# A Mamba-2 block and a gated feed-forward on one core: four first products ahead of the state products, three behind, and two of three copies by VectorE

## The chip, the cores and the metric

The kernel runs on one core of one Trainium2 chip. The metric is the device time of one execution in microseconds. The kernel before was timed in three runs: 345.36, 347.25 and 347.58 us, median 347.25 us. One further execution was taken with the hardware profiler. It took 349.48 us, of which 347.8 us are the profile's span (first to last instruction); all times inside the kernel are counted from the span's start.

## The reference

Two parts follow each other. The first is a state-space recurrence over 32 sequences (4 batches x 8 heads) of 768 positions, with head size 32 and state size 16; the second is a feed-forward over the resulting 3072 tokens of 256 channels.

```python
for c in range(nc):                        # chunks of 32 positions
    cum = np.cumsum(la, axis=-1)           # la = log(clip(a, 1e-6, 1))
    L = np.exp(cum[:, :, :, None] - cum[:, :, None, :]) * causal
    M = np.einsum('bhin,bhjn->bhij', Cc, Bc) * L
    y_intra = np.einsum('bhij,bhjd->bhid', M, xc)
    y_inter = np.einsum('bhin,bhnd->bhid', Cc, state) * np.exp(cum)[:, :, :, None]
    y[:, :, sl] = y_intra + y_inter
    state = decay_full * state + sum_j(B_j x_j * decay_from_j)
# tokens (3072, 256) = y, heads side by side
h = x @ w_in                               # 256 -> 2048
g = h * (1.0 / (1.0 + np.exp(-1.702 * h)))
out = g @ w_out                            # 2048 -> 256
```

The weights come as float64; the kernel makes float32 of their bits.

## The kernel before, in words

**Tiling.** The 3072 tokens are cut into six groups of 512. A group is two "pairs"; a pair is two chunks of 128 positions, each computed as two sides of 64. For each group the kernel makes yT, the recurrence's output with channels on partitions ([128, 2, 512]), then the hidden layer and the output. The code counts groups from 0 (g); this text says group 1 to group 6. In the loop over g from 2 to 4, the feed-forward of group g+1 is computed while the recurrence of group g+2 is prepared, so the three passes of that loop make the yT of groups 4, 5 and 6.

**The recurrence of one group** has these steps: `score` (the products of C and B into PSUM, tile cb, L677), `weigh` (VectorE multiplies the decay L by cb, L688), `finish` (the products y: first those with the carried state, L817, then those within the side, L831, in all 368 or 384 instructions of TensorE, half of them weight loads), and the copies of y from PSUM into yT. For groups 4 to 6 (`swap`, code groups above 2), the halves of the second side lie exchanged in PSUM, so three copies are needed: one of 128x512 (L866) and two of 64x512 (L864) which go from partitions 64 to 127 into 0 to 63 and the other way. All three are on ScalarE.

**The feed-forward** multiplies 2x2 blocks with seven products in place of eight. For each of eight steps j, the first layer has seven "first" products, which the code calls j.1 to j.7. Products 1, 6, 7, 4 add up in one PSUM tile X (L947), in that order, and ScalarE copies X out after 1, 6 and 7 (L952) and takes the silu after 4. Products 5, 2, 3 add up in Y (L957); VectorE adds the copies to Y (L1079: j.D after 5 and 2, and another one after 3), and ScalarE takes the silu of the sums (L924: j.S, j.T). `mix_g` (M0, M1 and so on; L915 to L917) makes the sums and differences of a finished step for the second layer, and P is one of the seven products of the second layer (L1052), added up over all j in the tile acc. Each such product is two weight loads and two matmuls in the profile.

**PSUM.** X and Y take turns in four banks. The tiles cb, y and acc take turns in one area of four banks: y can be written only when `weigh` has read cb, and acc only when the three copies have read y.

**What sets the order.** `run(g, steps)` emits the steps of a string from left to right, and `in_order` at the end fixes this order on each engine. Waits between engines come from the tiles that they share. The string around the change is the one of `more` in the loop over groups. In it s is `score`, w `weigh`, y `finish` with its copies, and `refill` starts the loads of the next pair: a memset of one element by VectorE (L267), behind which SP issues the DMAs of a (decay, from scratch), af, zC, zB, b and x. The a that it loads is read by VectorE's scan (`decay`, L419) at the end of the string.

Of the kernel before, what the change touches and what calls it, by code (L numbers as in the profile page):

```python
# [11 lines left out]
AF = mybir.ActivationFunctionType  # L12
# [4 lines left out]
P = 128  # L17
# [18 lines left out]
def kernel(  # L36
# [31 lines left out]
    nc = tc.nc  # L68
# [218 lines left out]
    for r in range(R):  # L287
        (nc.sync, nc.scalar)[r % 2].dma_start(
            out=az0[32 * r:32 * r + 32].rearrange("p k s -> p (k s)"),
# [493 lines left out]
    def finish(pairs, steps=range(2)):  # L783


        g, first = divmod(pairs[0], PG)
        early = pairs[0] < PG

        swap = g > 2
        if 0 in steps:  # L790
            if early:
                y = [bank(f"y0_{i}")[:, :2 * P].rearrange("p (k i) -> p k i", i=H) for i in range(4)]
                begun_y[0] = [[y[2 * t + i] for t in range(NK)] for i in range(2)], set()
            else:
                both = area(f"y{pairs[0]}")[:, :, :len(pairs) * 2 * H].rearrange(
                    "p (s t) (k i) -> p s t k i", s=2, i=H)
                begun_y[pairs[0]] = [[both[:, i, t] for t in range(NK)] for i in range(2)] + [both], set()
        y, begun = begun_y[pairs[0]]

        def begin(i, t, parts):  # L800
            new = not begun & {(i, t, q) for q in parts}
            begun.update((i, t, q) for q in parts)
            return new

        def inter(n, p, sides=range(2)):

            for k in range(2):
                for i in sides:
                    m = 2 * k + i
                    if (4 * p + m) % (2 * NC) == 0:  # L810
                        continue
                    old = state[p][:, m - 1] if m else state[p - 1][:, 3]
                    for r in range(R):
                        t = r // 2
                        half = r % 2 ^ (swap and i)
                        rows, to = slice(32 * r, 32 * r + 32), Q * D * half
                        nc.tensor.matmul(  # L817
                            out=y[i][t][to:to + Q * D, 2 * n + k], lhsT=old[rows],
                            rhs=st[p]["CsT"][rows, k, SIDES[i]],
                            start=begin(i, t, range(Q * half, Q * half + Q)), stop=early,  # L820
                            tile_position=(32 * r, to), skip_group_check=True)

        def intra(n, p):
            L = Ls[p]
            for h, k in [(h, k) for h in range(NH) for k in range(2)] if early else [
                    (h, k) for k in range(2) for h in range(NH)]:
                    for i, side in enumerate(SIDES):
                        t, q = divmod(h, HB)
                        if i and swap:
                            q = (q + Q) % HB  # L830
                        nc.tensor.matmul(  # L831
                            out=y[i][t][D * q:D * q + D, 2 * n + k], lhsT=rx[p][side, k, h],
                            rhs=L[side, k, h // Q, h % Q],
                            start=begin(i, t, (q,)), stop=not early, tile_position=(H * i, D * q),
                            skip_group_check=True)

        cols = slice(2 * first * P, 2 * (first + len(pairs)) * P)

        if first == 0:
            yT[g] = ffn.tile([P, NK, TG], FP32, tag="yT", name=f"yT{g}")  # L840
        if early:
            for n, p in enumerate(pairs):
                if n:
                    fan_all(PG)
                intra(n, p)
            for n, p in enumerate(pairs):
                for i in range(2):
                    inter(n, p, (i,))
            for t in range(NK):
                for i in range(2):  # L850
                    nc.scalar.activation(  # L851
                        yT[g][:, t, cols].rearrange("p (k s i) -> p s k i", s=2, i=H)[:, i], y[i][t],
                        AF.Copy)
        else:
            for step in steps:
                for n, p in enumerate(pairs):
                    (inter, intra)[step](n, p)
            if 1 not in steps:
                return
            o = yT[g][:, :, cols].rearrange("p t (k s i) -> p s t k i", s=2, i=H)  # L860
            for i in range(2):
                if i and swap:
                    for to, src in (SIDES, SIDES[::-1]):
                        nc.scalar.activation(o[to, i], y[2][src, i], AF.Copy)  # L864
                else:
                    nc.scalar.activation(o[:, i], y[2][:, i], AF.Copy)  # L866
        for p in pairs:
            state.pop(p - 1, None)
            st.pop(p)
            Ls.pop(p)  # L870
# [313 lines left out]
    to = area("cb0")  # L1184
# [99 lines left out]
    def run(g, steps, products=(), **do):  # L1284


        products = iter(products)
        for step in steps.split():
            if step == "P":
                product(*next(products))  # L1290
            elif step in do:
                do[step]()
            else:
                j, i = step.split(".")
                first(g, int(j), i)
        assert next(products, None) is None
# [52 lines left out]
    for g in range(2, NG):  # L1349
        n, p = (g + 1) * PG, (g + 2) * PG  # L1350
        more, most = g + 1 < NG, g + 2 < NG
        rows = [b for b in range(NB) if most and (g + 2) * CG <= b * NC < (g + 3) * CG]
        if most:
            load(p)
        run(g, "0.1 P P 0.6 P P 0.7 P 0.5 P 0.2 P 0.D", seven(g - 1, 6))
        def turn_third():
            if g == 2:
                turn_blocks(3)

        def start_third():  # L1360
            if g == 2:
                for k in n, n + 1:
                    since_start(k)

        def mask_third(k):
            if g == 2:
                mask_blocks(k)

        left = []
        run(g, "1.1 t 0.S P 0.4 P P 1.6 u P 0.3 b 0.T v P 1.5 P 1.7 1.2 P 1.D C", seven(g - 1, 7),  # L1370
            C=lambda: left.append(combine(g - 1)), t=turn_third, b=start_third,
            u=lambda: mask_third(n), v=lambda: mask_third(n + 1))
        def along():
            for r in rows:
                clip_rows(r)
                decay_rows(r)

        def refill():
            if most:
                spread(p, held=True)  # L1380
                for b in rows:
                    spread_rows(b)
                load(p + 1)
                spread(p + 1)

        if more:

            run(g, "2.1 1.S 1.4 1.3 2.6 2.5 2.2 2.7 1.T 3.1 s 2.D 2.S w 2.4 2.3 3.6 M0 3.5 3.2 3.7 2.T y "
                "refill 3.D 4.1 4.5 4.2 3.4 3.3 P P 4.6 P 3.S P 3.T M1 4.7 P P P 4.D M2",
                seven(g, 0), s=lambda: score((n, n + 1)), w=lambda: (weigh(n), weigh(n + 1)),  # L1390
                y=lambda: finish((n, n + 1)), refill=refill,
                M0=lambda: mix_g(g, 0), M1=lambda: mix_g(g, 1), M2=lambda: mix_g(g, 2))
            if most:
                decay(p)
        else:
            run(g, "2.1 1.S 1.4 1.3 2.6 2.5 2.2 2.7 1.T 2.D M0 3.1 3.5 2.4 3.6 2.S 2.3 Z 3.2 3.7 2.T 3.D M1",
                M0=lambda: mix_g(g, 0), M1=lambda: mix_g(g, 1), Z=lambda: left.pop()())
        for j in range(5 if more else 4, NF // 2):
            if j == 5:
                do = lambda: (mix_g(g, 3), turn_out(g - 1, 0))  # L1400
            else:
                do = lambda: mix_g(g, j - 2)
            run(g, steady(j, "o" if j == 6 else ""), seven(g, j - 4), M=do,
                o=lambda: turn_out(g - 1, 1))
            if most and j == 5:
                along()
            if most and j == 6:
                decay(p + 1)
            if most and j == 7:
                turn_blocks(g + 2)  # L1410
        k = NF // 2 - 1
        run(g, closing(k), seven(g, 4))
        if not more:
            for j in range(k - 1, k + 1):
                mix_g(g, j)
            break
        mix_g(g, 6)

        run(g, "P P A P P P P P", seven(g, 5), A=lambda: ahead(g + 1, p if most else None))
        mix_g(g, 7)  # L1420
# [33 lines left out]
```

## Time and profile before

| what | before |
|---|---|
| runs | 345.36, 347.25, 347.58 us; median 347.25 us |
| profiled execution | 349.48 us, span 347.8 us |
| TensorE busy | 340.9 us (98%) |
| TensorE weight loads busy | 272.9 us (78%, beside the matmuls) |
| VectorE busy | 256.1 us (74%) |
| ScalarE busy | 155.0 us (45%) |
| GpSimd busy | 14.4 us (4%) |
| granted TensorE clock, mean | 0.995 |

A busy share is an average over the whole span. What a stage is worth is read from that stage: from which wait ends last there. A line such as L947 is a line of the kernel; "PEld" is TensorE's weight load, "PE" its matmul, DVE is VectorE, ACT is ScalarE, SP issues most DMAs. An fp32 product shows as two matmuls and two weight loads in the trace.

### The profile page before, as it was taken

The page shows a single profiled execution, that of the slowest core. Times are in us where ns is not written, and L with a number is a line of the kernel's source. Part 1 is how long each engine was busy: PE and PEld are TensorE (multiplying, and loading weights), DVE is VectorE, ACT ScalarE, POOL GpSimd, SP SyncE. Part 2 cuts the span into 40 slices and gives each one's busy share as a digit, 9 for nine tenths or more (in the row PEclk, how much of TensorE's full clock was granted, in tenths as well). Part 3 has the DMA queues.
Part 4 walks back from the last instruction along what each step waited for, and adds up shares of the span by engine and source line. Part 5 has one row for each costly group of instructions (what it writes and reads, how often), then busy time and mean ns, then how long its engine had stood idle before and what let it go on. Part 6 is the DMA issues. An engine that isn't in the chain of part 4 may idle for free.

```text
span 347.8 us, 8119 instructions
## 1 busy us (share of the span) xinstructions
PE 340.9 (98%) x3378; PEld 272.9 (78%) x3378; DVE 256.1 (74%) x486; ACT 155.0 (45%) x353; POOL 14.4 (4%) x40
## 2 busy tenths in 40 slices
PE   8999999999999999979999999999999999999996
PEld 6644744555788888868888888888888888899996
DVE  6889999999998897837996567788464654465463
ACT  5797672316543315534442554432554321554320
POOL 6100111100000000000000000000000000000000
PEclk9999999999999999989999999999999999999999
DMA  6698899755736001346404016400000300000401
GB/s 163 153 285 195 243 206 132 149 79 110 115 95 114 0 2 30 47 123 106 78 19 59 0 62 121 80 0 3 0 4 3 60 2 0 0 2 0 62 0 61
DMA packets 89972, 25.75 MB, mean 74 GB/s; under 512 B 73392, under 2 KB 87216, under 8 KB 89936
## 3 DMA queue, kind: packets, MB, share of 16 engines
q1 hardware_dynamic: 89104, 24.72, 34.8%
q10 hardware_dynamic: 832, 0.52, 0.6%
q8 instruction: 26, 0.43, 0.5%
q14 instruction: 10, 0.08, 0.1%
HBM read 21.99 MB, written 3.24 MB: 73 GB/s over the span
## 4 chain that ended last, share of the span: by engine, by line
PE 98%; issue 1%; ACT 0%; DVE 0%
PE acc L1052 28%; PE X L947 19%; PE Y L957 14%; PE h L891 10%; PE o L989 8%; PE acc L1059 7%; PE y L831 3%; PE cb L677 2%; PE y L817 1%; PE A L708 1%; PE ab L551 1%; PE busy L463 1%; PE ab L545 0%; PE tp L594 0%; ACT yT L851 0%
## 5 line engine op out<-in xcount | busy, mean ns | idle before, releaser
L952 ACT ACTIVATE ac<-X 128x256 f32<-128x256 f32 x76 | 29.1, 383 | 82.9 <-PE X L947 82.5
L1079 DVE TENSOR_TENSOR gT<-Y,ac 128x512 f32<-128x512 f32 x38 | 26.2, 689 | 38.6 <-PE Y L957 34.6
L1052 PE MATMUL acc<-mg,mw 128*128 128x256 f32 x192 | 54.5, 379 | 0.0
L924 ACT ACTIVATE gT<-gT 128x512 f32<-128x512 f32 (+1 forms) x76 | 38.8, 518 | 25.8 <-DVE gT L1079 25.2
L947 PE MATMUL X<-my,mi 128*128 128x256 f32 x152 | 45.1, 379 | 0.0
L1052 PEld LDWEIGHTS acc<-mg,mw 128*128 128x128 f32 x192 | 36.5, 190 | 5.0
L1079 DVE TENSOR_TENSOR gT<-Y,b 128x256 f32<-128x256 f32 x38 | 15.9, 419 | 30.8 <-PE Y L957 30.7
L891 PE MATMUL h<-yT,w_in 128*128 128x512 f32 (+1 forms) x96 | 35.1, 523 | 0.5 <-ACT yT L851 0.5
L1052 PE MATMUL acc<-gT,w_out 128*128 128x256 f32 x128 | 35.5, 379 | 0.0
L947 PEld LDWEIGHTS X<-my,mi 128*128 128x128 f32 x152 | 28.1, 190 | 3.7
L891 PEld LDWEIGHTS h<-yT,w_in 128*128 128x128 f32 x96 | 18.1, 190 | 16.0 <-issue 12.7
L989 PE MATMUL o<-gT,w_out 128*128 128x512 f32 x64 | 28.3, 596 | 0.0
L915 DVE TENSOR_TENSOR mg<-gT 128x512 f32<-128x512 f32 x40 | 27.2, 680 | 0.0
L1052 PEld LDWEIGHTS acc<-gT,w_out 128*128 128x128 f32 x128 | 24.3, 190 | 3.3
L952 ACT ACTIVATE b<-X 128x256 f32<-128x256 f32 x38 | 14.6, 384 | 21.7 <-PE X L947 21.2
L947 PE MATMUL X<-yT,w_in 128*128 128x256 f32 x76 | 23.4, 392 | 0.0
L957 PE MATMUL Y<-my,mi 128*128 128x256 f32 x76 | 23.2, 387 | 0.0
L957 PE MATMUL Y<-yT,w_in 128*128 128x256 f32 x76 | 22.9, 383 | 0.0
L947 PE MATMUL X<-my,w_in 128*128 128x256 f32 x76 | 22.8, 383 | 0.0
L989 PEld LDWEIGHTS o<-gT,w_out 128*128 128x128 f32 x64 | 11.8, 190 | 13.6 <-issue 13.2
L957 PE MATMUL Y<-yT,mi 128*128 128x256 f32 x76 | 22.5, 379 | 0.0
L419 DVE TENSOR_TENSOR_SCAN L<-a,idents 128x1024 f32<-128x1024 f32 x9 | 20.5, 2277 | 0.0
(152 smaller groups left out, 549.9 us busy)
## 6 DMA issues: line engine op xcount, KB each, us to landing
a<-scratch SPq DMA_DIRECT2D x18, 256.0 KB, 5.2
bits<-in_moe_w_out_dram SPq DMA_DIRECT2D x8, 512.0 KB, 6.8
x<-in_x_dram SPq DMA_DIRECT2D x24, 128.0 KB, 3.6
out_dram<-ob SPq DMA_DIRECT2D x40, 64.0 KB, 2.0
bits<-in_moe_w_in_dram SPq DMA_DIRECT2D x8, 256.0 KB, 4.2
bits<-in_moe_w_in_dram SPq DMA_DIRECT2D x4, 512.0 KB, 9.7
b<-in_B_dram SPq DMA_DIRECT2D x20, 64.0 KB, 3.2
af<-in_a_dram SPq DMA_DIRECT2D x3, 384.0 KB
```

The costliest lines, as they stand in the source:

```text
L419: nc.vector.tensor_tensor_scan(out=L, data0=ra[p].rearrange("p k e -> p (k e)"), data1=idents.rearrange("p h i -> p (h i)"), initial=0.0, ...
L831: nc.tensor.matmul(out=y[i][t][D * q:D * q + D, 2 * n + k], lhsT=rx[p][side, k, h], rhs=L[side, k, h // Q, h % Q], start=begin(i, t, (q,)) ...
L891: nc.tensor.matmul(out=h[:, cols], lhsT=w_in[:, f, k], rhs=yT[g][:, k, cols], start=(k == 0 and c == 0), stop=(k == NK - 1), skip_group_ch ...
L915: nc.vector.tensor_tensor(out=t[:, 0:2], in0=B[:, :, 1], in1=B[:, 0], op=ALU.subtract)
L924: nc.scalar.activation(o, i, AF.Silu, scale=GELU_SCALE)
L947: nc.tensor.matmul(out=s["X"], lhsT=lhsT, rhs=rhs, start=i == "1", stop=i == "4", skip_group_check=True)
L952: nc.scalar.activation(copy, s["X"], AF.Copy)
L957: nc.tensor.matmul(out=o, lhsT=lhsT, rhs=rhs, start=s.pop("new", False), stop=i != "5", skip_group_check=True)
L989: nc.tensor.matmul(out=o[c], lhsT=w_out[:, c, f], rhs=gT[g, f // 2][:, f % 2], start=(f == 0), stop=(f == NF - 1), skip_group_check=True)
L1052: nc.tensor.matmul(out=acc[g][0][i][:, cols], lhsT=w, rhs=h[:, cols], start=(j == 0 and k == 0 and (i, 0) in begins), stop=(j == NF // 2 - ...
L1059: nc.tensor.matmul(out=o[k] if type(o) is list else o[:, cols], lhsT=h[:, cols], rhs=w, start=(j == 0 and (i, k) in begins), stop=(j == NF ...
L1079: nc.vector.tensor_tensor(out=o, in0=v, in1=w, op=ALU.add)
```

## The change

The string of the loop's passes with `more` is changed, and two of the copies of y go to another engine.

```diff
             for i in range(2):
                 if i and swap:
                     for to, src in (SIDES, SIDES[::-1]):
-                        nc.scalar.activation(o[to, i], y[2][src, i], AF.Copy)
+                        nc.vector.tensor_copy(out=o[to, i], in_=y[2][src, i])
                 else:
                     nc.scalar.activation(o[:, i], y[2][:, i], AF.Copy)
...
-            run(g, "2.1 1.S 1.4 1.3 2.6 2.5 2.2 2.7 1.T 3.1 s 2.D 2.S w 2.4 2.3 3.6 M0 3.5 3.2 3.7 2.T y "
-                "refill 3.D 4.1 4.5 4.2 3.4 3.3 P P 4.6 P 3.S P 3.T M1 4.7 P P P 4.D M2",
+            run(g, "2.1 1.S 1.4 1.3 2.6 2.5 2.2 2.7 1.T 3.1 s 2.D 2.S w 2.4 2.3 3.6 M0 3.5 3.2 3.7 2.T 4.1 3.D "
+                "4.5 4.2 4.6 y refill 4.7 3.4 3.3 P P P 3.S P 3.T M1 P P P 4.D M2",
```

Before, no product of step 4 stands ahead of y, and five first products (4.1, 4.5, 4.2, 3.4, 3.3) stand between y and the first P; 4.6 and 4.7 lie among the P. After, 4.1, 4.5, 4.2 and 4.6 stand ahead of y, and 4.7, 3.4 and 3.3 between y and the seven P in a row. The addition 3.D moves ahead of y, and so ahead of y's copies on VectorE; the refill's memset stays behind y, and so comes behind VectorE's two copies. Each of the three passes executes this string once; the refill loads in two of them (the last pass has nothing left to load).

## The prediction

> **What bounds the kernel now.** I read the page first. Its part 1 gives TensorE 340.9 us of a 347.8 us span, and the chain that ended last is 98% TensorE. So a gain must come out of the few microseconds in which TensorE stands still, and any new wait of TensorE adds to the span. The list of what TensorE waited for (second) is short:
>
> ```profile
> engine line waited for: us in total, times, longest us
> PE y L831 <- issue: 2.1, 2, 1.8
> PE busy L463 <- DVE ones L308: 1.1, 1, 1.1
> PE h L891 <- ACT yT L851: 0.5, 1, 0.5
> ```
>
> After 18 us TensorE never waits for another engine. One pause is inside the stage that is changed: 1.76 us of "issue" (nothing that the profile shows) in the state products y of group 4. Third, the busy times by stretch (length, then busy time of TensorE, its weight loads, VectorE, ScalarE, GpSimd; then the granted clock): from y's first weight load to the first weight load of acc, once for each of groups 4, 5, 6, and around the pause.
>
> ```profile
> 146.46:154.15 7.69, 5.93 (x195) 5.03 (x195) 2.06 (x6) 2.87 (x7) 0.00 (x0) 0.78 0.29 98
> 202.89:207.13 4.24, 4.24 (x195) 3.85 (x194) 2.07 (x6) 2.58 (x6) 0.00 (x0) 1.00 0.17 57
> 255.91:260.21 4.30, 4.30 (x203) 3.91 (x202) 2.05 (x5) 2.58 (x6) 0.00 (x0) 1.00 0.01 4
> ...
> 146.41:149.82 3.41, 1.65 (x118) 1.39 (x118) 2.12 (x6) 0.69 (x2) 0.00 (x0) 1.00 0.08 26
> 149.82:153.24 3.42, 3.42 (x72) 2.87 (x72) 0.00 (x0) 2.06 (x4) 0.00 (x0) 0.50 0.32 123
> ```
>
> Group 4 takes 7.69 - 4.27 = 3.42 us more than the other two (mean of 4.24 and 4.30). 1.76 us is the pause; the rest is the stretch behind it, in which the clock was granted at 0.50 for 3.42 us (half of that, 1.7 us). Fourth, the timeline of the same place in group 5 (start, length), where nothing goes wrong:
>
> ```profile
> 205.08 0.30 PEld L947 LDWEIGHTS X<-yT,w_in 128*128 128x128 f32 x2
> ...
> 205.19 0.60 ACT L866 ACTIVATE yT<-y 128x512 f32<-128x512 f32 x1 [1.50 <-PE y L831]
> ...
> 205.80 1.19 ACT L864 ACTIVATE yT<-y 64x512 f32<-64x512 f32 x2
> ...
> 207.13 0.84 PEld L1052 LDWEIGHTS acc<-gT,w_out 128*128 128x128 f32 x4
> ```
>
> acc takes the PSUM area that y held, so its first product needs the three copies. They end at 206.99; five first products (0.43 us each) cover them, and acc comes on time with 0.14 us to spare.
>
> **Part by part.** TensorE's matmuls are the same ones in another order: 0.
>
> *4.1, 4.5, 4.2, 4.6 ahead of y.* 4.6 adds to the bank that 4.1 wrote, so it waits until ScalarE has copied 4.1 out. On group 5's clock 3.7 starts at 202.37, so 4.1 stands at 202.80 and the weight load of 4.6 at 203.88. ScalarE begins the copy of 3.7 at 203.00, the silu 0.28 later, the copy of 4.1 some 0.32 after that (as at 199.16 and 199.48), so it ends at 203.60 + 0.38 = 203.98. At 196.55 a weight load follows such a copy (end 196.50) by 0.05. So 4.6 loads at 204.03, 0.15 late; of a delay of 0.05 nothing was lost there. I take +0.1 us for each of three groups (0 to 0.15). The other waits are met: 4.5 needs Y of 2 read by VectorE (ends 202.90, needed at 203.2); y needs the weighing, which ended 0.3 us before y starts now and so gets 1.7 us more.
>
> *Three products behind y, and the copies on two engines.* In the order that was built, VectorE's first copy waits for ScalarE's copy (both write yT), and acc's first product waits for VectorE's second. So the copies are still a chain of three. Let E be the first weight load behind y (205.08 in group 5). Today acc loads at E+2.05 and multiplies at E+2.26; two products less (0.86) put it at E+1.19 and E+1.40. The chain: ScalarE starts at E+0.11, ends at E+0.71; VectorE starts 0.04 later, as it does behind a ScalarE copy at 263.59 and 263.63. No row shows VectorE copying one operand from PSUM. Nearest rows, both ends:
>
> ```profile
> L1079 DVE TENSOR_TENSOR gT<-Y,ac 128x512 f32<-128x512 f32 x38 | 26.2, 689 | 38.6 <-PE Y L957 34.6 <-ACT ac L952 3.7
> ...
> L503 DVE TENSOR_SCALAR af<-af 128x768 f32<-128x768 f32 x3 | 1.6, 540 | 0.0
> L503 DVE TENSOR_SCALAR af<-af 128x256 f32<-128x256 f32 x1 | 0.3, 277 | 0.1
> ```
>
> L1079 reads PSUM over the same 512 columns: 0.69 us. L503 has one operand but reads SBUF: (540-277)/512 = 0.51 ns a column, so 0.41 us for 512. I take 0.69, since L1079 shares the source. In a run of such operations the next starts 0.08 before the last ends (263.63 and 264.24). So the second copy ends at E + 0.75 + 0.61 + 0.69 = E+2.05; plus 0.05 to the weight load and 0.21 to the matmul, E+2.31 against E+1.40: **+0.9 us** a group. Low end: 0.75 + 0.33 + 0.41 gives E+1.75, +0.35. High end: no overlap and a pause of 0.05 between the copies, E+2.46, +1.06. With the built chain a gain here is excluded. I use +0.95, nearer the high end because the two copies cross partition halves in opposite directions, which no row shows.
>
> [...]
>
> *ScalarE* loses 2 x 0.6 us a group. It waits 82.5 us for TensorE's X in all, so this is worth nothing.
>
> *VectorE* gains about 1.4 us a group in a gap that is there (idle 2.52 us ahead of 3.3's addition at 207.55).
>
> *The refill moves behind the copies.* Its first instruction is a memset on VectorE (204.37 now) that lets SP issue the DMAs: two a, af, zC, zB, b, x, two a, in SP's order. It goes to about y's end + 2.2, some 4.7 us later on the clock of group 5. The first a lands 4.0 to 4.8 us after its issue, the second is issued 0.6 to 1.3 later; so they are there some 5 to 6 us after the memset, while the scan (L419) could start 4.2 us after it. It waits 0.5 to 1.6 us, and VectorE with it: behind it stand Be, 4.3's addition (215.40 now) and 5.D's, ahead of which VectorE idles 1.29 us today. The silu behind 4.3's addition ends at 216.27, and ScalarE's next copy starts at 217.97 after 1.69 us idle. So both idle gaps cover it: 0, with up to 0.3 us if the second a is slow. The second pair of a is used at 225.28, 10 us behind its issue; b and x behind that.
>
> *The pause in group 4.* One 16 KB packet of instructions arrived for TensorE in this stretch at 147.2 (26 such packets in the run, for 6,800 of its instructions, so about 256 in each), and TensorE resumed 2.6 us later. Counting TensorE's instructions in the trace, the short "issue" at 15.6 us and this one lie 2,816 = 11 x 256 apart. So I read the pause as a wait for the next block of instructions: y's 368 need only 6 ns each, the others 108. The block edge was 235 instructions into y; with 16 more ahead of y it is 219 in, but four products (1.7 us) later. TensorE would stand there 0.1 us or not at all, and the half clock goes: **-3.4 us** (0 to -3.4, as a pause elsewhere can't be excluded). Late next is the wait of acc.
>
> Sum for the profiled execution: 3 x 0.95 + 3 x 0.1 - 3.4 = -0.25, so 349.48 becomes 349.2 us.
>
> **Against the median.** The runs are 345.36, 347.25, 347.58. The profiled time without the pause would be 349.48 - 3.4 = 346.1, close to the lowest run; the other two lie 2 us above it, as if they held a pause. So I put the pause into two of three runs, take the lowest as the time without it, and add what the change costs: 345.36 + 3.15 = **348.5 us**, 0.4% above the median.
>
> **Rivals.**
> *1. The new gaps drop the clock (slower).* The row 146.41:149.82, 48% busy, was followed by half clock. At 16.70:20.12 TensorE was busy 2.91 of 3.42 us (85%), and the clock stayed. A gap of 1 us makes 71%, between them. If that suffices, each gap costs 1.7 us more: 348.5 + 3 x 1.7 = 353.6, or 350.2 with one. It decides once the gap passes some length between 0.5 and 1.76 us. For it: y's small tiles lie in the same stretch. Against: 71% is nearer to the 85. [...]
> *2. The pause is only in the profiled execution, or comes back elsewhere.* Then nothing is won: 347.25 + 3.15 = 350.4. For it: the same stage of groups 5 and 6 has no pause. Against: the spread of the runs.
> *3. The copies cost little*, at L503's rate: 345.36 + 3 x (0.35 + 0.1) = 346.7; a little faster than now. Against: PSUM rows of VectorE are no quicker than SBUF's.
> That the copies run side by side, as the change reads, is excluded by the built waits.
>
> **Chances.** Forecast 0.58 (its own range 347.3 to 350.2: gaps of 0.35 to 1.06, base 345.4 to 346.5), rival 1 0.17, rival 2 0.15, rival 3 0.10. Range: 346.3 to 352.0, which leaves out most of rival 1's three drops. This kernel's runs differ by 0.6%, so about 1% can be told from none: slower by over 1% means above 350.7 (rival 1 but for its single drop, a third of rival 2, the forecast's tail: 0.27); faster by over 1% means under 343.8, which only a larger gain than any I can name would give, 0.04; within 1% 0.69.
>
> **What the profile after would show.** TensorE's list gains "acc" waiting for VectorE's yT copy, three times, 0.9 to 1.0 us each; VectorE's two copies of 0.69 us start behind ScalarE's; y has no "issue" above 0.3 us and the clock row no 8 at 148 us. A clock of 0.5 behind any of the three gaps is rival 1. Copies of 0.4 us, or copies that start with ScalarE's, would prove the chain wrong; a pause at another block edge would prove the gain wrong.

## The result, and the profile after

The changed kernel takes 348.53 us in the median of 22 runs (348.10 to 349.94). The kernel before, run 22 times too (the three runs of above among them), takes 346.36 us (345.03 to 349.42). The ratio is 1.0056, with a 95% interval from 1.0036 to 1.0077: slower by about half a per cent, which is surely not zero. Here and below, a ratio leaves out runs over 1.5% above the fastest of the same kernel, which is one run, of experiment 8. Lowest run against lowest run, the change costs 3.07 us. The forecast was 348.5 us, with 3.15 us of cost on the kernel before without its pause.

The two sets of runs differ in kind as well. Of the 22 runs of the kernel before, 11 lie between 345.0 and 346.0 us, and the others reach up to 349.4. Of the changed kernel's 22, 18 lie between 348.1 and 348.9.

The profiled execution of the changed kernel took 348.45 us, span 346.7 us. What TensorE waited for (engine, tile and line, what it waited for, then us in total, times, longest) now begins:

```profile
PE acc L1052 <- DVE a L267: 1.4, 2, 0.7
...
PE acc L1052 <- DVE yT L864: 0.7, 1, 0.7
```

The "issue" of y is gone. Three waits of acc are new, of 0.7 us each. Two are put down to the memset L267 only because it is the last thing VectorE did; it stands right behind the copies. The group of the copies themselves (durations min/median/max, then forms, then what VectorE waited for ahead of them):

```profile
L864 DVE COPY yT<-y x6: 683/688/694, 150.6 to 259.3; 64x512 f32<-64x512 f32 x6
...
  ACT yT L866: 7.7, 3
```

So each copy takes 0.69 us, and ahead of each of the three pairs VectorE stands idle until ScalarE's copy is done. The timeline of group 5 (start, length, then idle time and its releaser in brackets) shows the chain:

```profile
203.83 0.30 PEld L947 LDWEIGHTS X<-my,mi 128*128 128x128 f32 x2
...
203.93 0.60 ACT L866 ACTIVATE yT<-y 128x512 f32<-128x512 f32 x1 [1.81 <-PE y L831]
...
204.57 1.39 DVE L864 COPY yT<-y 64x512 f32<-64x512 f32 x2 [2.56 <-ACT yT L866]
...
206.10 1.10 PE L1052 MATMUL acc<-gT,w_out 128*128 128x256 f32 x4 [0.71 <-DVE a L267]
```

With E = 203.83, the first weight load behind y, ScalarE copies from E+0.10 to E+0.70, VectorE from E+0.74 to E+2.13, and acc multiplies at E+2.27. The three products behind y are through long before, at E+1.55.

### The profile page after: what moved, and what is told of

Read it like the earlier page. It is cut to its first block, busy times and chain, and to the rows that moved or that the text cites. A ratio compares the mean times of both kernels' runs of the same rounds, so it can differ in the third digit from the quotient of the medians.

```text
span 346.7 us, 8113 instructions
## 1 busy us (share of the span) xinstructions
PE 339.3 (98%) x3378; PEld 270.7 (78%) x3378; DVE 259.9 (75%) x492; ACT 151.7 (44%) x347; POOL 14.3 (4%) x40
## 4 chain that ended last, share of the span: by engine, by line
PE 94%; DMA 2%; DVE 1%; SPq 1%; ACT 1%; issue 0%; ACTq 0%
PE acc L1052 28%; PE X L947 18%; PE Y L957 14%; PE h L891 10%; PE o L989 8%; PE acc L1059 7%; PE y L831 3%; PE cb L677 2%; PE y L817 2%; DVE yT L864 1%; PE A L708 1%; DMA x<-in_x_dram 1%; SPq L150 1%; DMA zC<-in_C_dram 1%; ACT yT L866 1%
## 5 line engine op out<-in xcount | busy, mean ns | idle before, releaser
L1079 DVE TENSOR_TENSOR gT<-Y,ac 128x512 f32<-128x512 f32 x38 | 26.1, 688 | 31.5 <-PE Y L957 30.8
L1079 DVE TENSOR_TENSOR gT<-Y,b 128x256 f32<-128x256 f32 x38 | 15.9, 420 | 20.5 <-PE Y L957 20.3
L947 PE MATMUL X<-yT,w_in 128*128 128x256 f32 x76 | 22.6, 380 | 0.0
L989 PEld LDWEIGHTS o<-gT,w_out 128*128 128x128 f32 x64 | 11.8, 190 | 13.6 <-issue 13.2
```

The source lines that it names most:

```text
L947: nc.tensor.matmul(out=s["X"], lhsT=lhsT, rhs=rhs, start=i == "1", stop=i == "4", skip_group_check=True)
L989: nc.tensor.matmul(out=o[c], lhsT=w_out[:, c, f], rhs=gT[g, f // 2][:, f % 2], start=(f == 0), stop=(f == NF - 1), skip_group_check=True)
L1079: nc.vector.tensor_tensor(out=o, in0=v, in1=w, op=ALU.add)
```

## The experiments

**1. The order alone.** The changed string is kept; all three copies go back to ScalarE.

```diff
-                        nc.vector.tensor_copy(out=o[to, i], in_=y[2][src, i])
+                        nc.scalar.activation(o[to, i], y[2][src, i], AF.Copy)
```

> The order of the change with all three copies on ScalarE (the first half of the change alone). Theory A, acc waits for the chain of copies: ScalarE's three copies end 1.91 us behind the first weight load behind y (as in group 5 of before), so the first matmul of acc comes at about 2.06 instead of 1.40, a loss of 0.74 to 0.77 us a group, 2.3 us in all: about 347.8 us, 0.6 to 0.7 below the changed kernel. Theory B, the loss comes from VectorE being loaded and the refill being late: both go, so 345.5 us.

Measured: 348.1 us in the median (5 runs, 347.89 to 348.39), beside 346.05 of the kernel before; ratio 1.0051 [1.0028, 1.0074]. Theory A holds. The timeline of group 5:

```profile
204.13 0.30 PEld L947 LDWEIGHTS X<-my,mi 128*128 128x128 f32 x2
...
204.85 1.20 ACT L864 ACTIVATE yT<-y 64x512 f32<-64x512 f32 x2
...
206.09 1.13 PE L1052 MATMUL acc<-gT,w_out 128*128 128x256 f32 x4 [0.40 <-ACT yT L864]
```

acc now multiplies at E+1.96 (E = 204.13). So the shorter cover is the larger part of the loss, whoever copies; ScalarE alone is 0.3 us quicker through the same three copies than the two engines are. In the median this run is 0.4 us below the changed kernel, where 0.6 to 0.7 was forecast.

**2. VectorE's copies written down first.** If only the place of the copies in the code ties VectorE to ScalarE, this should free them.

```diff
-            for i in range(2):
+            for i in (1, 0) if swap else (0, 1):
```

> The changed kernel with VectorE's two copies written down ahead of ScalarE's copy; in the built order VectorE's copies then wait for TensorE alone. Theory A (chain of copies): VectorE starts with ScalarE, ends 1.50 us behind the first weight load behind y, acc's first matmul at 1.65 instead of 2.28, the loss falls from 0.96 to about 0.33 us a group: about 346.6 us. Theory B (load of VectorE, late refill): VectorE has the same work and the refill is earlier by only 0.6 us, so no more than 0.5 us is won: 348 us.

Measured: 348.77 us (4 runs); ratio 1.0072 [1.0050, 1.0094]. A miss for A: nothing was won. The tie only turned round; ScalarE's copy now starts when VectorE's end:

```profile
204.38 1.39 DVE L864 COPY yT<-y 64x512 f32<-64x512 f32 x2 [1.92 <-PE y L831]
...
205.87 0.60 ACT L866 ACTIVATE yT<-y 128x512 f32<-128x512 f32 x1 [3.29 <-PE Y L957]
...
206.52 0.70 PE L1052 MATMUL acc<-gT,w_out 128*128 128x256 f32 x2 [0.68 <-ACT yT L866]
```

The profile names 3.3 as the last releaser of ScalarE, because TensorE's last product ahead of 205.87 is 3.3. But in the trace ScalarE's copy waits for VectorE too, and VectorE's second copy ends at 205.77, 0.10 us ahead of it.

**3. The copies cut by channel half.** Each engine writes one half of the channels in yT, and reads PSUM banks that the other doesn't.

```diff
-            for i in range(2):
-                if i and swap:
+            if swap:
+                for t in (1, 0):
+                    copy = nc.vector.tensor_copy if t else nc.scalar.copy
+                    copy(out=o[:, 0, t], in_=y[2][:, 0, t])
                     for to, src in (SIDES, SIDES[::-1]):
-                        nc.vector.tensor_copy(out=o[to, i], in_=y[2][src, i])
-                else:
+                        copy(out=o[to, 1, t], in_=y[2][src, 1, t])
+            else:
+                for i in range(2):
                     nc.scalar.activation(o[:, i], y[2][:, i], AF.Copy)
```

> As the run with VectorE first, but the copies are cut by halves of the channels: VectorE makes three copies of 256 columns for one half, ScalarE three for the other. Theory A: both end about 1.25 to 1.4 us behind the first weight load behind y, acc's first matmul at about 1.5 instead of 1.40: a loss of 0.1 to 0.2 us a group, 345.7 to 346.1 us in every run. If the pause of the kernel before does not come back in this order, its median is below that of the kernel before (346.4) by 0.3 to 0.7 us; if the pauses come by chance in any order, its runs spread from 345.5 to 349.5 as those of the kernel before do.

Measured: 350.03 us (6 runs, 349.53 to 354.33); ratio 1.0128 [1.0088, 1.0167]. A miss again, and a worse one: six small copies, still one engine behind the other.

```profile
204.73 0.43 DVE L864 COPY yT<-y 128x256 f32<-128x256 f32 x1 [1.92 <-PE y L831]
205.17 0.86 DVE L866 COPY yT<-y 64x256 f32<-64x256 f32 x2
...
206.12 0.37 ACT L864 COPY yT<-y 128x256 f32<-128x256 f32 x1 [3.19 <-DVE yT L866]
206.50 0.74 ACT L866 COPY yT<-y 64x256 f32<-64x256 f32 x2
```

So it is not the overlap of what they write or of the banks they read. What is left in common are the tile yT that both write and the PSUM tile y that both read; run 4 tells them apart.

**4. The cost of the chain taken away.** VectorE's copies keep engine, shape, place in the order and target, but read the resident weights. Half of yT in groups 4 to 6 is then not computed.

```diff
-                        nc.vector.tensor_copy(out=o[to, i], in_=y[2][src, i])
+                        nc.vector.tensor_copy(out=o[to, i], in_=w_in[src, :2].rearrange(
+                            "p t k (c e) -> p t (k c) e", c=2))
```

> The changed kernel, with VectorE's two copies reading the resident weights instead of y (so half of yT in groups 4 to 6 is wrong; that part of the computation is left out). The copies keep their engine, their shape and their place, but nothing of y hangs on them: acc's first product waits for ScalarE's 0.6 us copy alone. Theory A (the chain ScalarE, VectorE, VectorE ahead of acc is the whole loss): acc's first product starts on its scheduled E+1.40 in groups 4 to 6, no wait of acc for a copy above 0.1 us, and the time comes down by 2.5 to 2.9 us to 345.3 to 345.8, ratio to before 0.996 to 0.999. Theory B (moving four products ahead of y costs by itself: the refill, the copies of 4.1 and 4.6, the scan): stays at 347 or more.

Measured: 345.83 us (10 runs) beside 345.86; ratio 0.9995 [0.9979, 1.0011]. The time came down by all that the change had cost. acc starts where the order puts it (E = 203.29):

```profile
201.51 0.86 DVE L864 COPY yT<-w_in 64x512 f32<-64x512 f32 x2
...
203.29 0.30 PEld L948 LDWEIGHTS X<-my,mi 128*128 128x128 f32 x2
...
204.69 0.81 PE L1053 MATMUL acc<-gT,w_out 128*128 128x256 f32 x3
```

That is E+1.40, and nothing of TensorE's list names acc. Two things follow. Moving four products and 3.D costs nothing that these runs can tell. And VectorE's copies wait for nobody here, though they write the same yT: the tie is in the reading of y. The late refill is not tested by this run, as its memset follows the copies and so comes early too, at 202.42, where the changed kernel has it at E+2.19; run 6 has it late.

**5. The copies alone.** The string of before, two copies by VectorE.

```diff
-                        nc.scalar.activation(o[to, i], y[2][src, i], AF.Copy)
+                        nc.vector.tensor_copy(out=o[to, i], in_=y[2][src, i])
```

> The order of the kernel before, with the two copies on VectorE behind ScalarE's (the second half of the change alone). Theory A: the copies end 2.13 us behind the first weight load behind y, acc's first matmul at 2.28, against 2.26 in the kernel before: 0 to 0.1 us a group, so the same as the kernel before within 0.3 us in its runs without a pause (345.3 to 345.9), and the pauses stay (median about 346.5). Theory B: half of the loss or more, 347 us and above.

Measured: 350.77 us (4 runs: 348.85, 350.36, 351.27, 351.17); ratio 1.0136 [1.0109, 1.0163]. Theory A is missed. The number lies in Theory B's open range, but the trace shows a wait that neither had named. The list of what TensorE waited for, and group 5's timeline:

```profile
PE Y L957 <- DVE gT L1079: 2.7, 3, 0.9
```

```profile
202.85 1.39 DVE L864 COPY yT<-y 64x512 f32<-64x512 f32 x2 [1.40 <-ACT yT L866]
...
204.26 0.69 DVE L1079 TENSOR_TENSOR gT<-Y,ac 128x512 f32<-128x512 f32 x1
...
205.00 0.70 PE L957 MATMUL Y<-yT,mi 128*128 128x256 f32 x2 [0.90 <-DVE gT L1079]
```

The wait isn't acc's. In the old order 3.D comes after y, so its addition queues on VectorE behind the two copies, and the product 3.3, which writes the bank that this addition reads, waits for it; acc then multiplies at E+3.43 (205.54), where the kernel before has E+2.26. That is a reading of one trace, of the run of 348.85 us; the next run checks it. Why the other three are 1.5 to 2.4 us longer still is open.

**6. The same with 3.D ahead of y.** The copies of 5, and one word of the string moved.

```diff
-... 3.5 3.2 3.7 2.T y refill 3.D 4.1 4.5 4.2 3.4 3.3 P P ...
+... 3.5 3.2 3.7 2.T 3.D y refill 4.1 4.5 4.2 3.4 3.3 P P ...
```

> The kernel before with two of three copies by VectorE, as in the earlier run of that, but 3.D's addition written ahead of y, so that it does not queue behind the copies. Five products stay behind y. Theory A (the extra loss of that earlier run was 3.D's addition behind the copies): 3.3 no longer waits 0.9 us for VectorE; acc's first product starts at E+2.3 against a scheduled 2.2, so a loss of 0.1 to 0.2 us per group, in sum 0.3 to 0.6: 346.3 to 347.2 in the median beside a before of 346.4, ratio 1.000 to 1.003. Theory B (the loss there was the copies themselves): stays near 349 to 350, ratio 1.010 or more.

Measured: 345.98 us (10 runs) beside 345.86; ratio 1.0014 [0.9991, 1.0037]. The loss is gone, a little more than forecast. The chain is as long as in the changed kernel (E = 201.56, acc at E+2.28), but five products take E+2.26:

```profile
202.30 1.39 DVE L864 COPY yT<-y 64x512 f32<-64x512 f32 x2 [0.80 <-ACT yT L866]
...
203.84 0.89 PE L1052 MATMUL acc<-gT,w_out 128*128 128x256 f32 x3
```

Run 6, the changed kernel and run 4 together: with five products behind y the two-engine chain costs nothing that these runs can tell; with three it costs 2.7 us (348.53 against 345.83); with three and no chain, again nothing.

**7. One product ahead of y, five behind, copies by ScalarE.** The candidate for a kernel better than both: the cover is kept, and something slow stands ahead of y.

```diff
-... 2.T y refill 3.D 4.1 4.5 4.2 3.4 3.3 P P 4.6 P 3.S ...
+... 2.T 4.1 y refill 3.D 4.5 4.2 4.6 3.4 3.3 P P P 3.S ...
```

> The kernel before, three copies by ScalarE, with one product (4.1) ahead of y and five behind it (4.5 4.2 4.6 3.4 3.3): the cover behind y stays 5 products, but a product stands between the score and y. Theory A (five products cover ScalarE's three copies, E+1.96 against E+2.2; a product ahead of y lengthens the stretch of slow instructions ahead of the 256-instruction block edge by 0.43 us and so takes most pauses): no wait of acc, median 345.2 to 345.9, ratio 0.996 to 0.999, and few runs above 346.5. Theory B (pauses come by chance or from DMA traffic): the same spread as before, 345.0 to 349.4, median 346.0 to 346.6.

Measured: 345.98 us (12 runs, 345.35 to 347.99) beside 345.86; ratio 1.0008 [0.9991, 1.0025]. No wait of acc, as forecast, but no gain, and the median lies between the ranges of the two theories. 2 of 12 runs lie above 346.5, and 5 of 29 of the kernel before, which left little to gain. So whether one product ahead of y thins out the long runs is not shown.

**8. Where the instruction blocks begin.** The kernel before with 120 small filler matmuls in place of its four wide ones, ahead of everything (112 in the expectation is a slip).

```diff
-    keep_busy(4, 0)
+    keep_busy(0, 120)
```

> The kernel before with other filler matmuls ahead of the first group (112 instead of 4 ones' worth of other shape), which change nothing behind them but shift TensorE's stream by 224 instructions, so that in group 4 a block of 256 instructions begins some 11 instructions into y and ends inside it: the whole block goes by in 1.6 us of 6 ns instructions. Theory A (the pause in y is TensorE waiting for its next block of instructions, which takes about 3.5 us to arrive): a gap of 1.5 to 2.5 us of kind issue at about instruction 267 of y of group 4 in nearly every run, with a window of half clock behind it in most: 347.0 to 349.5, median 1 to 3 us above before, and few runs below 346. Theory B (chance, or DMA traffic): the distribution of before.

Measured: 352.61 us in the median of three runs (350.57 to 354.53; a fourth took 358.96) beside 345.86; ratio 1.0190 [1.0143, 1.0237]. In the trace TensorE's stream is 464 instructions longer, not 224, so the edges fell 27 and 283 instructions into y of group 4. The gap in y of group 4 came, the window of half clock behind it did not. TensorE's list:

```profile
PE y L831 <- issue: 3.0, 3, 1.4
PE busy L455 <- issue: 1.8, 1, 1.8
```

Counted in the trace, the gaps begin on instructions 449, 1217, 4033 and 5057: each is 193 mod 256, as is the pause of before (3521). They are 1.77, 0.24, 1.32 and 1.43 us long, the last two in y of groups 4 and 5. But the sum explains only part of the time, so the fillers themselves needed a control.

**9 and 10. A whole block into y in three groups, and the control.** 36 small fillers make the stream longer by 128; four make it as long as before.

```diff
-    keep_busy(4, 0)
+    keep_busy(0, 36)      # the other run: keep_busy(0, 4)
```

> The kernel before with 36 small filler matmuls in place of 4 wide ones ahead of everything: 128 more instructions on TensorE, and nothing else moved. The edges of the 256-instruction blocks move by 128, so that a whole block lies in the short instructions of y in each of groups 4 to 6 (1.5 us from edge to edge by the trace of before, against 4.4 us there now). Theory A (TensorE waits for its next block, which takes some 4 us to come): gaps of kind issue of 1.5 to 2.6 us in each of the three groups, starting on an instruction with number 193 mod 256, 4.5 to 8 us together: 350 to 354, ratio 1.012 to 1.025. Theory B (the earlier filler run lost its time by its longer start alone, and gaps come by chance): within 1 us of before.

> The control to the last run: 4 small filler matmuls in place of the 4 wide ones, the same number of instructions as before, so that the block edges stay where they are. Both theories: the time of before within 0.5 us (345.4 to 346.6), ratio 0.998 to 1.002. If it is slower by more than 0.5 us, the shorter warm-up at the start is what the filler runs lose.

Measured: 359.41 us with 36 (4 runs; ratio 1.0382 [1.0327, 1.0436]) and 349.25 us with four (10 runs, 346.59 to 349.94; ratio 1.0061 [1.0030, 1.0092]), beside 345.89. The control failed as a control: it loses time by itself, 3.4 us between the medians and 1.0 to 3.2 by the interval of the ratio, with no pause. Its start says where. The tile "rows" of the run with four, and of the kernel before:

```profile
L529 PE MATMUL rows<-cum,whose x4: 630/710/790, 12.7 to 13.3; 32*128 32x256 f32 x4
```

```profile
L529 PE MATMUL rows<-cum,whose x4: 374/426/478, 10.3 to 10.6; 32*128 32x256 f32 x4
```

Without the wide fillers the same matmuls take 0.71 us in place of 0.43 and come later. The profile's clock row shows full speed there, but the trace's first record of a granted clock lies at 18.8 us in this run and at 6.5 us in the kernel before, and the row counts the time ahead of that record as full: it measures nothing there. The run with 36 loses that too, and beyond it 10 us; 8.5 of them are five pauses of 1.36 to 2.06 us, each again on an instruction 193 mod 256.

**11. The same 128 instructions with the wide fillers kept.**

```diff
-    keep_busy(4, 0)
+    keep_busy(4, 32)
```

> The kernel before with 32 small filler matmuls ahead of its 4 wide ones, which stay: again 128 more instructions on TensorE, with the start's warm-up kept. Theory A (the five pauses of the run with 36 small ones, 1.36 to 2.06 us each and 8.5 together, come from where the block edges lie; 3.4 us of that run came from the start, as its control lost them too): the same pauses on instruction 193 mod 256, and 353 to 357, ratio 1.021 to 1.033. Theory B (the pauses hang on the cold start): within 1.5 us of before.

Measured: 359.28 us (4 runs) beside 346.73; ratio 1.0365 [1.0332, 1.0398]. Theory A by mechanism, above its range by size. TensorE's list:

```profile
PE y L831 <- issue: 4.4, 3, 1.6
PE y L817 <- issue: 2.9, 1, 2.9
PE o L989 <- issue: 1.7, 1, 1.7
```

Five pauses, of 2.85, 1.65, 1.64, 1.44 and 1.33 us, each on an instruction 193 mod 256; three are in y of groups 4 to 6. They sum to 8.9 us. The fillers take 1.1, and the first 30 us have a mean clock of 0.94, which is 1.8 us more: 11.8 of the 12.4 us that lie between its profiled execution (358.28 us) and the 345.9 us of an undisturbed one. So in these runs such pauses begin on the edges, and a shift of the edges brings them about.

**12. Does the refill delay the block?** The kernel before, with its refill behind the first two P.

```diff
-                "refill 3.D 4.1 4.5 4.2 3.4 3.3 P P 4.6 P 3.S P 3.T M1 4.7 P P P 4.D M2",
+                "3.D 4.1 4.5 4.2 3.4 3.3 P P refill 4.6 P 3.S P 3.T M1 4.7 P P P 4.D M2",
```

> The kernel before with its refill (a memory set and the transfers of the next pair's inputs) moved behind the first two products of acc, some 3 us later; the block edges stay. In the profiled run of before a block took 5.8 us to come where 3.1 to 4.3 us are usual. Theory A (the refill's transfers delay that block): no pause in y, hardly a run above 346.5, median 345.2 to 345.8. Theory B (the delay has nothing to do with the refill): about as many runs above 346.5 as before has beside it, and the same median within 0.4 us.

Measured: 346.16 us (12 runs, 345.20 to 349.87) beside 346.73; ratio 0.9987 [0.9952, 1.0022]. 5 of 12 runs lie above 346.5, and 9 of 17 of before: theory B by the count, though the medians lie 0.57 us apart where it had 0.4. Its profiled execution (349.68 us) was one of the long ones, and its delay is another one: TensorE's list, and the stretch in which the waits lie with the one behind it (columns as in the windows of the prediction).

```profile
PE A L708 <- DMA x<-in_x_dram: 1.1, 2, 0.6
```

```profile
81.84:85.25 3.41, 1.98 (x74) 1.04 (x80) 3.10 (x8) 0.72 (x2) 0.00 (x0) 1.00 0.83 123
85.25:88.67 3.42, 3.42 (x67) 2.06 (x52) 2.54 (x8) 1.58 (x8) 0.00 (x0) 0.50 0.37 110
```

x came late, TensorE was busy 58% of 3.41 us, and the clock was granted at 0.50 in the next 3.42 us. So long runs have at least two causes, the pause in y and late x, and in both profiled executions half clock added to it.

## Why the prediction was right

**No work added on TensorE: right.** With the chain taken away (run 4) the order costs nothing: from y of group 5 to y of group 6 TensorE takes 53.04 us, and 53.02 in the kernel before.

**4.6 behind ScalarE's copy of 4.1, +0.1 a group: right in kind, too large.** In group 5 the weight load of 4.6 stood 0.16 us for that copy, against the 0.15 worked out, and its two matmuls took 0.62 us in place of 0.59. Of the 0.1 us, at most 0.03 is found.

```profile
201.01 0.30 PEld L947 LDWEIGHTS X<-my,mi 128*128 128x128 f32 x2 [0.16 <-ACT ac L952]
201.09 0.62 PE L947 MATMUL X<-my,mi 128*128 128x256 f32 x2
```

**The chain of three copies, +0.95 a group: right.** Worked out: acc at E+2.31 against E+1.40. Measured: E+2.27 in the changed kernel, E+1.40 without the chain, so 0.87 to acc's first product. From y of group 5 to y of group 6 the difference is 0.95 (53.99 us against run 4's 53.04), and 3 x 0.95 is 2.85, beside 2.70 between the medians of the two. The prediction's high end adds up to E+2.44 and +1.04, where it has 2.46 and 1.06. VectorE's copy took the 0.69 us of L1079, not the 0.41 of L503, and so rival 3 falls.

VectorE's copy of 256 columns from PSUM took 0.43 us (run 3) and that of 512 took 0.69, so 1.0 ns a column against L503's 0.51 from SBUF; in run 4 the two copies of 512 columns from SBUF took 0.86 us together. Two copies of 0.69 took 1.39 us, with no overlap, where the prediction had worked with 0.08 us of it. That puts the chain in the upper half of the range that the prediction gave. Its reason for standing there, that the two copies cross the partition halves, was an estimate that no run bears out: in run 3 VectorE's two copies of 256 columns that cross took 0.86 us, and the one that doesn't cross 0.43.

**Why the copies are tied: wrong in its reason.** The prediction said that both write yT. In run 4 VectorE's copies write the same yT without waiting for ScalarE's (at 201.51, where ScalarE's starts at 203.40), and in run 3 reading other banks does not free them (ScalarE starts at 206.12, 0.09 us behind VectorE's end): the common tile which ties them is y, read from PSUM by both. It was right that this order excludes a gain.

**ScalarE's relief and VectorE's load, 0: right here,** as TensorE's list has no new row above 0.3 us but acc's, which are the chain. Run 5 shows how near it was: with 3.D left behind y, the same 1.4 us on VectorE made 3.3 wait 0.9 us a group and acc's first product come 1.17 us later. The prediction had taken the gap ahead of 3.3's addition as free, and did not say that moving 3.D is what made it so.

**The refill, 0: right in the end, its wait too small.** The scan was forecast to wait 0.5 to 1.6 us; it waited 1.98 in group 5 and 2.4 at most.

```profile
212.03 2.29 DVE L419 TENSOR_TENSOR_SCAN L<-a,idents 128x1024 f32<-128x1024 f32 x1 [1.98 <-DMA a<-scratch]
...
214.77 0.42 DVE L1079 TENSOR_TENSOR gT<-Y,b 128x256 f32<-128x256 f32 x1
```

TensorE's list shows no row that hangs on it. Run 6 has the memset as late (203.76, E+2.20) and loses nothing that these runs can tell.

**The pause, -3.4 in the profiled execution: right.** The changed kernel's page has no pause and a full clock row, and 349.48 became 348.45 us, where 349.2 was forecast (0.5 of the difference lies in the start, where the first products with the carried state came at 15.9 in place of 16.5 us). That the pause is a wait for the next block of 256 instructions was an inference from two gaps; runs 8, 9 and 11 bear it out. In their traces 13 pauses of over 1 us begin on an edge, and in each TensorE resumes 2.3 to 2.9 us behind the start of a 16 KB packet of instructions, as it did before (2.6). Counted from edge to edge, TensorE of the kernel before goes through the block ahead of the edge in y in 4.4 to 4.5 us in groups 5 and 6, and in 3.8 us in group 4 (the trace of run 12, whose edges lie alike); where it had to wait, in runs 8 and 9, 3.1 to 4.3 us passed with the pause included (5.2 in one case of run 9). So group 4 had nothing to spare. In the changed kernel the block takes 5.5 to 6.2 us.

An edge inside y is not enough, though: in run 8 one whole block went by in 1.6 us with no pause (77.34 to 78.94), where two packets had come during the block ahead of it. And the profiled pause of before was longer than usual: 5.8 us passed from edge to edge. Its packet set off at 147.19, 3.2 us behind the edge, where run 12 and the changed kernel have 0.2 and 0.4. What held it back is open; it is not the refill, whose first transfer was issued at 148.02, and between 143.7 and 147.0 no DMA packet moved at all.

**The sum: right, its closeness in part luck.** Without the 0.3 us for 4.6 the cost is 2.85 us. The 11 runs of before under 346 us have a median of 345.71, so the base of 345.36 was 0.35 too low. The two errors cancel to within 0.05 us. The low end of the forecast's own range, 347.3, does not follow from its terms (345.4 + 3 x 0.35 = 346.5).

**Rival 1 (the new gaps drop the clock) did not come:** gaps of 0.7 us left the clock at full. Nor did the clock turn near 71% busy, the share with a gap of 1 us that the prediction weighed. In the traces the clock changes on a grid of 3.41 us, and each drop inside the kernels lasts one step of it (149.82 to 153.24 in the kernel before). Ahead of the four drops inside the kernels, TensorE was busy 48% of a step (before), 44% (run 9), 28% (run 11) and 58% (run 12). But steps of 51% and 53% (run 9) and of 55% and 52% (run 11) were followed by full clock, the last with a pause of 1.64 us:

```profile
154.45:157.86 3.41, 1.77 (x129) 1.53 (x119) 1.18 (x4) 0.13 (x1) 0.00 (x0) 1.00 0.22 75
157.86:161.28 3.42, 3.42 (x17) 3.01 (x17) 1.16 (x3) 2.30 (x5) 0.00 (x0) 1.00 0.63 156
```

So neither the share nor the length of a gap decides alone in these traces, and what does is open. In run 3, with three gaps of 1.1 us, five of six executions stayed at full clock and one had a mean of 0.994 and took 4.3 us more than the others; where that one lost its clock is not on record. **Rival 2** (the pause only in the profiled execution) is half true, as far as the times tell: half of the runs of before lie under 346 us, as if free of it, but only the profiled execution shows the pause itself. The longer runs of before are why lowest to lowest shows 3.07 us but the medians 2.2.

## What to carry to other kernels

Count the work that stands between the last write of a PSUM area and its next owner: here that cover, not the busy share of the copying engine, decided whether the copies cost anything (nothing that the runs can tell with five products of cover, 2.7 us with three). Before splitting copies of one PSUM tile over two engines, look whether the second engine waits for the first; here it always did (its copy began 0.03 to 0.10 us behind the end of the first's), so the split made the chain longer (acc at E+2.27 in place of E+1.96), and what is left is a PSUM tile for each engine, which no run here tried. And look behind the moved instruction on its new engine: 3.D's addition, one step further down, was worth as much as the whole chain (54.18 us from y of group 5 to y of group 6 in run 5, 53.10 in run 6).

## What the runs showed of the hardware that was not expected

- The place of the 256-instruction edges alone cost over 10 us of 346 in run 11. With 128 more small matmul instructions ahead of everything, 1.1 us of work, the kernel took 359.28 us; pauses make 8.9 us of its profiled loss, and half clock behind one of them 1.8. A change that only shifted TensorE's stream was then not neutral here, and of the places tried here the kernel before has the best.
- Without the wide filler matmuls at the start the kernel took 349.25 us in the median against 345.89: matmuls ran at 0.71 in place of 0.43 us some 12 us into the execution, while the clock row of the page, which has no record there, showed full speed.
- Three waits of 1.4 us in sum within 3.41 us, in run 12, were followed by half clock over the next 3.4 us, while single pauses of 1.3 to 1.7 us inside runs 8, 9 and 11 were not.
